# Narrower scores for the first query block of each sequence in a fused attention and MLP kernel

## The chip, the cores and the metric

The kernel runs on one core of one Trainium2 chip. The metric is the device time of one launch in microseconds. The engines are named as in the profile: PE is TensorE (matmuls), PEld its weight loads, DVE is VectorE, ACT is ScalarE, POOL is GpSimd, SP is the queue that issues most of the DMAs. Everything is computed in fp32 accuracy.

## The reference

Four sequences of 768 positions, eight heads of 64, attend to a window of the last 128 positions and to the first four positions ("sinks"). The result goes through an MLP with a softplus.

```python
scores = scale * np.matmul(q, k.transpose(0, 1, 3, 2))
is_sink = pos[None, :] < int(n_sink)
rel = pos[:, None] - pos[None, :]
keep = is_sink | ((rel >= 0) & (rel < int(window)))
scores = np.where(keep, scores, -1000000000.0)
a = np.exp(scores - np.max(scores, axis=-1, keepdims=True))
a = a / (np.sum(a, axis=-1, keepdims=True) + 1e-09)
attn = np.matmul(a, v)
# then, per position, with x of 512 numbers:
h = x @ w_in
g = np.maximum(h, 0.0) + np.log1p(np.exp(-np.abs(h)))
out = g @ w_out
```

Queries come in blocks of 128. A block needs the keys of its own block (up to the diagonal), of the block before it (beyond the diagonal), and the sinks. The first block of a sequence has no block before it.

## The kernel before

Work is cut into 12 chunks of 256 queries, three to a sequence: chunk 0, 3, 6 and 9 begin a sequence (`self.first`). A chunk has eight heads, counted on through the chunks, so that head 24 is the first of chunk 3. Each head has two query blocks, j = 0 and j = 1, and passes through these steps: `load` (DMA), `split` (rounded part and rest of q and k), `scores`, `softmax`, `normalise`, `weights_t` (transposes of the weights and their masking on GpSimd into `pt`), `values` (product with v and with the sinks' values `vs`), `out`. Every four heads, `sink_weights` and `sink` transpose the weights on the sinks (tile `ts`, line 281). The MLP's `up`, `softplus`, `gate`, `residue` and `down` of a chunk run eight heads later, between the attention steps of the next one.

The keys of a chunk lie in SBUF as key block, 8 sink keys, key block, 8 sink keys, key block. For query block j the scores are one stretch of 264 columns: the block before, the sinks, the own block. The softmax then copies the own block's scores over those of the block before wherever key position is not beyond the query's (`c.diag`), and goes on with 136 columns, 128 keys and 8 sinks. For the first block of a sequence, the layout holds block 0 twice, in the place of the block before too.

The chunks 0 and 1 are "exact": q and k are plain fp32, and a product is one matmul in the program, two records in the profile (line 227). From chunk 2 on q and k are split into parts rounded to fp32r, and a block's scores are two matmuls that add up in PSUM (lines 230 and 231). The rest of the kernel's large matmuls (lines 327, 333, 459, 496 to 498) are of the rounded kind as well; those of the MLP are the bulk of the work.

```python
mv = slice(j * KW, j * KW + 2 * P + NS)      # KW = 136, P = 128, NS = 8
nc.tensor.matmul(s[:], hi[:, st], hi[:, mv], start=True, stop=False)
nc.tensor.matmul(s[:], hi[:, st], kl[:, mv], start=False, stop=True)
...
nc.vector.copy_predicated(self.s[h, j][:, :P], c.diag[:], self.s[h, j][:, KW:])
```

The order on TensorE and on the SP queue is the order in which the program is written: a list by hand (`START`) for the first two chunks, and then one round per head with fixed strings of steps (`STEADY`). The rounds of a sequence's first heads also build the sinks' values on GpSimd (`sinks`). In the first 100 us or so the MLP's weights arrive, issued from ScalarE's queue, and are unpacked from 64-bit words and split by ScalarE, VectorE and GpSimd (lines 403, 48, 50, 52, 56), in the same queues as the attention's steps.

A score tile is a PSUM tile of 264 columns; two pools hold two buffers each, so scores of a later head wait until the softmax has read those of an earlier one.

Of the kernel before, what the change touches and what calls it, by code (L numbers as in the profile page):

```python
# [22 lines left out]
P = 128  # L23
NB = S // P
NS = 8
KW = P + NS
CH = 2
# [95 lines left out]
class _Attention:  # L123
# [93 lines left out]
    def scores(self, h):  # L217
        c, nc = self.c, self.c.nc
        ops = self.heads.pop(h)
        for j in range(CH):  # L220
            pool, tag = (c.ps_h, "h") if self.chunk == 0 and h % 2 else (c.ps_s, "s")
            s = pool.tile([P, 2 * P + NS], F32, tag=tag, name=f"s{self.chunk}_{h}_{j}")
            mv = slice(j * KW, j * KW + 2 * P + NS)
            st = slice(KC + j * P, KC + j * P + P)
            if self.exact:
                q, k = ops
                nc.tensor.matmul(s[:], q[:, j * P : j * P + P], k[:, mv], start=True, stop=True)  # L227
            else:
                hi, kl = ops
                nc.tensor.matmul(s[:], hi[:, st], hi[:, mv], start=True, stop=False)  # L230
                nc.tensor.matmul(s[:], hi[:, st], kl[:, mv], start=False, stop=True)  # L231
            self.s[h, j] = s

    def softmax(self, h):
        c, nc, chunk = self.c, self.c.nc, self.chunk
        g, hh = h // G, h % G
        if hh == 0:
            self.a[g] = c.ap.tile([P, G, CH, KW], F32, tag="a", name=f"a{chunk}_{g}")
            self.rc[g] = c.sp.tile([P, CH, G], F32, tag="rc", name=f"rc{chunk}_{g}")
        sm = c.sp.tile([P, CH], F32, tag="sm", name=f"sm{chunk}_{h}")  # L240
        self.sm[h] = sm
        for j in range(CH):
            nc.vector.copy_predicated(self.s[h, j][:, :P], c.diag[:], self.s[h, j][:, KW:])  # L243
        for j in range(CH):
            a = self.a[g][:, hh, j]
            k = (chunk * H + h) * CH + j
            nm = c.stats[:, k : k + 1]
            m = c.masks[min(self.i0 + j, 2)]
            nc.vector.tensor_tensor_reduce(a, self.s.pop((h, j))[:, :KW], m[:], -SCALE, BIG, ALU.add, ALU.min, nm)  # L249
            nc.scalar.activation(a, a, AF.Exp, bias=nm, scale=-1.0, accum_out=sm[:, j : j + 1])  # L250
# [653 lines left out]
```

## Time and profile before

| | |
|---|---|
| device time, median of 3 runs | 740.09 us (737.24 to 740.62) |
| span of the profiled execution | 735.7 us, 13883 instructions |
| TensorE busy | 699.7 us, 95% |
| VectorE busy | 552.6 us, 75% |
| ScalarE busy | 446.1 us, 61% |
| GpSimd busy | 400.7 us, 54% |
| score matmuls, lines 227, 230, 231 | 64, 160 and 160 records |
| copies, line 243 | 192, 49.1 us busy |

The profiled execution's own time is its span from the first to the last instruction, 735.7 us; no time around it is given with the profile. A row of a group view has the line, the engine, the operation, the tiles, the shapes and the count, then busy time and mean time of one record, then the idle time of the engine before these records and what ended it. Busy times on TensorE count overlapping records once and a record's length includes its way through the array, so the distance between two starts, from the view in order of time, says what a matmul costs. A piece of the chain of waits has its start, its length, the engine, tile and line.

### The profile page before, as it was taken

To read this page: it belongs to the slowest core of one execution; us is meant where nothing else is said; L and a number is where in the kernel's file an instruction comes from. 1 tells how busy PE (TensorE), PEld (TensorE's weight loads), DVE (VectorE), ACT (ScalarE), POOL (GpSimd) and SP (SyncE) were. 2 spreads that over 40 slices of the span, in tenths; PEclk is the share of its full clock that TensorE was granted. 3 is DMA by queue.
4 is the path that set the end of the run, shared out by engine and by line. 5 is a ranking of instruction groups with operands and counts; after the bars stand their busy time and mean duration, and the time that the engine had idled before them with its cause. 6 is when DMAs were issued, how large, how long until landed. Compare 5 with 4: busy or idle time off the path is not lost.

```text
span 735.7 us, 13883 instructions
## 1 busy us (share of the span) xinstructions
PE 699.7 (95%) x4489; PEld 624.8 (85%) x4489; DVE 552.6 (75%) x1608; ACT 446.1 (61%) x1098; POOL 400.7 (54%) x773
## 2 busy tenths in 40 slices
PE   4788899989999999998999999998999999999996
PEld 3567688979899999997899999997999999999995
DVE  5899997867877877876977887886887877754331
ACT  3577865655666666665666666665766756644331
POOL 4866476565555665665655655556655565553110
PEclk9899999999999999999999999999999999999999
DMA  8877611411321321321321322322222222100001
GB/s 291 310 255 235 187 40 48 126 46 44 98 67 49 105 61 54 93 63 42 92 74 49 95 69 57 95 60 61 62 74 77 83 61 76 58 13 0 30 1 35
DMA packets 40876, 63.22 MB, mean 86 GB/s; under 512 B 4634, under 2 KB 22362, under 8 KB 40794
## 3 DMA queue, kind: packets, MB, share of 16 engines
q1 hardware_dynamic: 36042, 45.47, 21.2%
q10 hardware_dynamic: 4752, 16.77, 6.5%
q8 instruction: 38, 0.62, 0.4%
q14 instruction: 44, 0.36, 0.2%
HBM read 55.93 MB, written 6.29 MB: 85 GB/s over the span
## 4 chain that ended last, share of the span: by engine, by line
PE 83%; DVE 6%; POOL 4%; ACT 3%; DMA 1%; issue 1%; ACTq 0%; SPq 0%; POOLq 0%; DVEq 0%
PE h L459 34%; PE acc L496 11%; PE acc L498 11%; PE acc L497 11%; PE x L333 6%; PE t L297 2%; PE s L230 2%; PE s L231 2%; PE x L327 2%; PE s L227 1%; ACT a L250 1%; POOL a L264 1%; DMA wo71r<-w 1%; POOL pt L308 1%; PE ts L281 1%
## 5 line engine op out<-in xcount | busy, mean ns | idle before, releaser
L459 PE MATMUL h<-xh,wi 128*128 128x256 f32 x1536 | 254.6, 289 | 0.0
L459 PEld LDWEIGHTS h<-xh,wi 128*128 128x128 f32 x1536 | 212.3, 192 | 1.2 <-issue 0.3
L459 PE MATMUL h<-xl,wi 128*128 128x256 f32 x768 | 154.9, 284 | 0.0
L496 PE MATMUL acc<-wo,gh 128*128 128x512 f32 x384 | 153.7, 400 | 0.0
L498 PE MATMUL acc<-wo,gl 128*128 128x512 f32 x384 | 151.7, 395 | 0.7 <-DVE gl L56 0.7
L497 PE MATMUL acc<-wo,gh 128*128 128x512 f32 x384 | 151.5, 395 | 0.0
L52 POOL TENSOR_SCALAR gh<-mt 128x512 fp32r<-128x512 f32 x91 | 56.5, 621 | 166.7 <-DVE mt L474 165.4
L466 ACT ACTIVATE mt<-h 128x512 f32<-128x512 f32 x96 | 57.2, 596 | 114.2 <-PE h L459 114.2
L459 PEld LDWEIGHTS h<-xl,wi 128*128 128x128 f32 x768 | 120.0, 192 | 0.0
L264 POOL TENSOR_SCALAR a<-a,rc 128x128 f32<-128x128 f32 x180 | 71.9, 411 | 87.1 <-DVE rc L257 78.8
L250 ACT ACTIVATE a<-a,stats 128x136 f32<-128x136 f32 x192 | 75.9, 396 | 39.1 <-DVE stats L249 39.0
L474 DVE SCALAR_TENSOR_TENSOR mt<-h,mt 128x512 f32<-128x512 f32 x96 | 65.9, 687 | 42.4 <-ACT mt L468 28.2
L498 PEld LDWEIGHTS acc<-wo,gl 128*128 128x128 f32 x384 | 72.8, 189 | 17.8 <-DVE gl L56 1.2
L496 PEld LDWEIGHTS acc<-wo,gh 128*128 128x128 f32 x384 | 72.8, 190 | 12.9 <-issue 0.4
L497 PEld LDWEIGHTS acc<-wo,gh 128*128 128x128 f32 x384 | 72.9, 190 | 9.3
L56 DVE TENSOR_TENSOR gl<-mt,gh 128x512 fp32r<-128x512 f32 x96 | 70.5, 734 | 4.4 <-POOL gh L52 4.0
L467 ACT ACTIVATE mt<-mt 128x512 f32<-128x512 f32 x96 | 60.8, 633 | 3.1
L468 ACT ACTIVATE mt<-mt 128x512 f32<-128x512 f32 x96 | 60.7, 633 | 3.0
L351 DVE TENSOR_TENSOR xt<-x,xt 64x256 f32<-64x256 f32 x80 | 33.2, 415 | 38.9 <-ACT xt L48 38.9
L243 DVE COPY_PREDICATED s<-diag,s 128x128 f32<-128x128 int32 x192 | 49.1, 289 | 15.4 <-PE s L231 11.9
L48 ACT CAST qkh<-qk 128x656 fp32r<-128x656 f32 x80 | 59.3, 741 | 0.4 <-DMA qk<-qk 0.4
L333 PE MATMUL x<-pt,vv 128*128 128x256 f32 (+1 forms) x216 | 48.7, 328 | 7.9 <-POOL pt L311 7.9
(183 smaller groups left out, 1234.9 us busy)
## 6 DMA issues: line engine op xcount, KB each, us to landing
qk<-qk SPq DMA_DIRECT2D x160, 164.0 KB, 3.0
vr<-v SPq DMA_DIRECT2D x32, 192.0 KB, 2.8
out<-o SPq DMA_DIRECT2D x24, 256.0 KB, 2.3
q<-q SPq DMA_DIRECT2D x8, 256.0 KB, 4.7
vr<-v SPq DMA_DIRECT2D x16, 128.0 KB, 2.1
k<-k SPq DMA_DIRECT2D x8, 200.0 KB, 4.9
wi00r<-w ACTq DMA_DIRECT2D x1, 511.8 KB
wi01r<-w ACTq DMA_DIRECT2D x1, 511.8 KB
```

What stands on the lines that cost most here:

```text
L48: nc.scalar.copy(out, in_)
L56: (nc.vector if eng == "V" else nc.gpsimd).tensor_tensor(out, a, b, ALU.subtract)
L250: nc.scalar.activation(a, a, AF.Exp, bias=nm, scale=-1.0, accum_out=sm[:, j : j + 1])
L264: (nc.vector if eng == "V" else nc.gpsimd).tensor_scalar(a, a, rc[:, j : j + 1], 0.0, ALU.mult, ALU.add)
L333: nc.tensor.matmul(x[:, :, o], w, pt[:, :, m], start=False, stop=n == 2, skip_group_check=True)
L459: nc.tensor.matmul(h[:, j], wt, x, start=k == 0, stop=k >= len(prods) - 2, skip_group_check=True)
L467: nc.scalar.activation(t[:], t[:], AF.Exp, scale=-1.0)
L468: nc.scalar.activation(t[:], t[:], AF.Ln, bias=1.0)
L474: nc.vector.scalar_tensor_tensor(t[:], h[:], 0.0, t[:], ALU.max, ALU.add)
L496: nc.tensor.matmul(acc[:], gh[:, j, q], wh, start=f == 0, stop=False, skip_group_check=True)
L497: nc.tensor.matmul(acc[:], gh[:, j, q], wl, start=False, stop=False, skip_group_check=True)
L498: nc.tensor.matmul(acc[:], gl[:, j, q], wh, start=False, stop=f == 2 * FP - 1, skip_group_check=True)
```

## The change

For the first query block of a chunk that begins a sequence, the matmuls compute 136 columns, the first copy of block 0 and the sinks, and the copy of the second over the first is left out. The PSUM tile keeps its size; loads, layout, masks and the softmax's remaining steps are as they were.

```diff
             s = pool.tile([P, 2 * P + NS], F32, tag=tag, name=f"s{self.chunk}_{h}_{j}")
-            mv = slice(j * KW, j * KW + 2 * P + NS)
+            w = KW if self.first and j == 0 else 2 * P + NS
+            mv = slice(j * KW, j * KW + w)
             st = slice(KC + j * P, KC + j * P + P)
+            o = s[:, :w]
             if self.exact:
                 q, k = ops
-                nc.tensor.matmul(s[:], q[:, j * P : j * P + P], k[:, mv], start=True, stop=True)
+                nc.tensor.matmul(o, q[:, j * P : j * P + P], k[:, mv], start=True, stop=True)
             else:
                 hi, kl = ops
-                nc.tensor.matmul(s[:], hi[:, st], hi[:, mv], start=True, stop=False)
-                nc.tensor.matmul(s[:], hi[:, st], kl[:, mv], start=False, stop=True)
+                nc.tensor.matmul(o, hi[:, st], hi[:, mv], start=True, stop=False)
+                nc.tensor.matmul(o, hi[:, st], kl[:, mv], start=False, stop=True)
             self.s[h, j] = s
...
-        for j in range(CH):
+        for j in range(1 if self.first else 0, CH):
             nc.vector.copy_predicated(self.s[h, j][:, :P], c.diag[:], self.s[h, j][:, KW:])
```

On TensorE, at the first head of chunk 3 (tile names are `s` with head, block and a number; `hi` and `kl` are the tiles `qkh` and `kl`), the order before was:

```order
L230 MATMUL s_0_0_1884<-qkh_0_1776 128x264
L231 MATMUL s_0_0_1884<-kl_0_1779,qkh_0_1776 128x264
L230 MATMUL s_0_1_1887<-qkh_0_1776 128x264
L231 MATMUL s_0_1_1887<-kl_0_1779,qkh_0_1776 128x264
L496 MATMUL acc_0_1700<-wo_691,gh_2_1714 128x512
```

and with the change it is:

```order
L232 MATMUL s_0_0_1876<-qkh_0_1768 128x136
L233 MATMUL s_0_0_1876<-kl_0_1771,qkh_0_1768 128x136
L232 MATMUL s_0_1_1879<-qkh_0_1768 128x264
L233 MATMUL s_0_1_1879<-kl_0_1771,qkh_0_1768 128x264
L498 MATMUL acc_0_1692<-wo_683,gh_2_1706 128x512
```

The places are the same; two of four score matmuls are narrower. Every later line number of the program moves by two, so that line 243 becomes 245. On VectorE, at the first head of the program, before (L249 is the masked reduction of a block's scores):

```order
L243 COPY_PREDICATED s_0_0_172<-diag,s_0_0_172 128x128
L243 COPY_PREDICATED s_0_1_174<-diag,s_0_1_174 128x128
L249 ISA a_0_178,stats<-s_0_0_172,mask_141 128x136
L249 ISA stats 128x1
L249 ISA a_0_178,stats<-s_0_1_174,mask_142 128x136
```

and with the change:

```order
L245 COPY_PREDICATED s_0_1_174<-diag,s_0_1_174 128x128
L251 ISA a_0_178,stats<-s_0_0_172,mask_141 128x136
L251 ISA stats 128x1
L251 ISA a_0_178,stats<-s_0_1_174,mask_142 128x136
L251 ISA stats 128x1
```

One copy of two is gone, and the remaining one still stands ahead of the reduction of block j = 0. On the other engines and on the DMA queues nothing moves.

## The prediction

> **What bounds the kernel now.** I read four views: the page's busy times and chain of waits, then stretches of time, then single TensorE records, then the start of the chain. The page first:
>
> ```profile
> PE 699.7 (95%) x4489; PEld 624.8 (85%) x4489; DVE 552.6 (75%) x1608; ACT 446.1 (61%) x1098; POOL 400.7 (54%) x773
> PE 83%; DVE 6%; POOL 4%; ACT 3%; DMA 1%; issue 1%; ACTq 0%; SPq 0%; POOLq 0%; DVEq 0%
> ```
>
> TensorE carries the end. But the average hides two regimes, which the view by stretches shows (columns: start and end, length, then PE, PEld, DVE, ACT, POOL busy with counts, granted clock, DMA share, GB/s):
>
> ```profile
> 10.00:20.00 10.00, 5.85 (x23) 4.28 (x24) 5.80 (x29) 6.24 (x23) 3.76 (x10) 0.78 1.01 377
> 17.00:20.00 3.00, 2.62 (x9) 2.05 (x10) 1.53 (x5) 2.89 (x9) 0.00 (x0) 0.50 1.03 413
> 20.00:30.00 10.00, 9.09 (x43) 5.87 (x42) 9.23 (x38) 5.26 (x20) 8.74 (x12) 0.88 0.84 310
> 30.00:40.00 10.00, 7.02 (x34) 4.47 (x32) 9.19 (x31) 5.49 (x19) 8.32 (x15) 1.00 0.78 276
> 90.00:100.00 10.00, 10.00 (x73) 8.81 (x72) 9.80 (x26) 6.77 (x15) 4.18 (x8) 1.00 0.19 52
> ```
>
> From 10 to 20 us no engine is full: the engines wait for each other in turn, partly at half clock (0.50). From 20 us VectorE is full (9.23, 9.19) and GpSimd nearly. From about 90 us TensorE never stops. So a shorter matmul pays in the first 20 us and after 90 us, a dropped VectorE copy pays before 90 us and almost nowhere after.
>
> **The change part by part.** It shortens the scores of query half j=0 in chunks 0, 3, 6 and 9 from 264 to 136 columns and drops their copies; no instruction changes place. The rows concerned, by shape:
>
> ```profile
> L230 PE MATMUL s<-qkh 128*128 128x264 f32 x160 | 43.7, 292 | 0.0
> L231 PE MATMUL s<-kl,qkh 128*128 128x264 f32 x160 | 42.6, 286 | 0.0
> L227 PE MATMUL s<-k,q 128*128 128x264 f32 x64 | 20.5, 457 | 9.2 <-DMA q<-q 5.6 <-DVE stats L249 2.5 <-PE s L227 0.6
> L459 PE MATMUL h<-xh,wi 128*128 128x256 f32 x1536 | 254.6, 289 | 0.0
> L243 DVE COPY_PREDICATED s<-diag,s 128x128 f32<-128x128 int32 x192 | 49.1, 289 | 15.4 <-PE s L231 11.9
> ```
>
> *Rounded scores (chunks 3, 6, 9): 3 chunks x 8 heads x 2 products = 48 matmuls.* A record's mean (292 ns) includes its latency; what it costs is the distance to the next start:
>
> ```profile
> 183.12 0.29 PE L230 MATMUL s<-qkh 128*128 128x264 f32 x1
> 183.24 0.29 PE L231 MATMUL s<-kl,qkh 128*128 128x264 f32 x1
> 183.37 0.29 PE L230 MATMUL s<-qkh 128*128 128x264 f32 x1
> 183.49 0.28 PE L231 MATMUL s<-kl,qkh 128*128 128x264 f32 x1
> 183.62 0.40 PE L496 MATMUL acc<-wo,gh 128*128 128x512 f32 x1
> 183.85 0.40 PE L497 MATMUL acc<-wo,gh 128*128 128x512 f32 x1
> 184.08 0.39 PE L498 MATMUL acc<-wo,gl 128*128 128x512 f32 x1
> ```
>
> Four of 264 columns take 0.50 us, 0.125 each (0.12 to 0.13), and one of 512 takes 0.23. That is (0.23 - 0.125) / 248 = 0.42 ns a column, so 128 columns fewer would give 0.054 back, if streaming were all. It isn't: each matmul has a weight load of its own, and the loads have a width and a pace too:
>
> ```profile
> L230 PEld LDWEIGHTS s<-qkh 128*128 128x128 f32 x160 | 30.5, 190 | 0.9 <-issue 0.3
> L327 PEld LDWEIGHTS x<-sk,vsf 128*64 128x64 f32 x32 | 3.2, 139 | 7.7 <-ACT sk L48 3.3 <-issue 2.6 <-DVE xl L56 1.3
> 144.15 0.19 PEld L230 LDWEIGHTS s<-qkh 128*128 128x128 f32 x1
> 144.25 0.19 PEld L231 LDWEIGHTS s<-kl,qkh 128*128 128x128 f32 x1
> 144.38 0.19 PEld L230 LDWEIGHTS s<-qkh 128*128 128x128 f32 x1
> ```
>
> 64 columns of weights fewer make a load 190 - 139 = 51 ns shorter, 0.8 ns a column; 128 columns then hold the loader some 0.10 us, and the closest pair here, behind a short matmul, is 0.10 to 0.11 apart. The next load starts with the matmul before it, so a matmul of 136 columns still lasts until the next weights are in. I expect a spacing of 0.117, 0.008 less than now: 48 x 0.008 = 0.4 us. The bounds: streaming alone, 48 x 0.054 = 2.6 us; nothing, if 0.125 is already the load's pace. I take the value next to the load rows, since the 0.10 to 0.11 is a measured distance of these same loads. The Trainium skill, page "TensorE: Matmul & The Clock Gate", section "LDWEIGHTS (loading the stationary operand)", says a load costs its columns divided by 1.2 GHz, which is an estimate of 107 ns here; by that rule the gain would be 48 x (125 - 107) = 0.9 us at most. The trace agrees with the pace (0.10 to 0.11).
>
> *Exact scores (chunk 0, 8 heads).* A plain fp32 product is two records (64 for 32 products). Warm, four records fit between these two starts, 0.89 / 4 = 0.22 each:
>
> ```profile
> 24.12 1.06 PE L227 MATMUL s<-k,q 128*128 128x264 f32 x4
> 25.01 0.38 PE L297 MATMUL t<-ident,a 128*128 128x128 f32 x2
> ```
>
> and these are the places where they, and the copies of chunk 0, stand on the chain of waits:
>
> ```profile
> 5.62 3.61 PE s L227 x8
> 9.86 2.04 PE s L227 x8
> 13.82 0.39 DVE s L243 x2
> 16.28 0.39 DVE s L243 x2
> 17.38 0.58 PE ts L281 x2
> 17.96 1.76 PE s L227 x4
> 20.15 1.76 PE s L227 x4
> 27.64 0.38 DVE s L243 x2
> ```
>
> At half clock a record is 1.76 / 4 = 0.44. Scaled by 136/264 it becomes 0.227, saving 0.213; warm 0.22 becomes 0.12 (the load's pace again), saving 0.10. On the chain: heads 0 and 1, four cold records, 0.85; heads 2 and 3, four warm, 0.40; a copy of head 3 and one of head 4, half of 0.39 each, 0.39. That is 1.64 us by 17 us, where the first stretches show no other engine full, so I count all of it. Behind it stand heads 5 and 6 (four cold records, 0.85) and one copy (0.19), but there VectorE and GpSimd are full and have work of their own; I count 0.2 of this 1.04. Term: 1.8 us. Upper bound 2.7 (all); lower bound 0, if a weight transfer or GpSimd holds the next step anyway. In the new VectorE order the copy of j=1 still stands ahead of the j=0 reduction, so j=0 is not released earlier by itself.
>
> *Dropped copies of chunks 3, 6, 9: 24.* Records overlap, so each frees 0.39 / 2 = 0.195 us, 4.7 us together. I cost them at nothing: TensorE's 10.00 of 10 covers them. If that cover were gone they would give up to those 4.7. One kind of place has none, where TensorE waits for a chain with VectorE in it:
>
> ```profile
> 185.86 0.40 DVE s L243 x2
> 192.48 0.62 PE L333 MATMUL x<-pt,vv 128*128 128x512 f32 x2 [0.39 <-POOL pt L311]
> 162.68 1.01 PE L333 MATMUL x<-pt,vv 128*128 128x256 f32 x2 [2.38 <-POOL pt L311]
> ```
>
> The wait of 0.39 at 192.48 hangs on a chain that passes head 29's copies; it and its twin a batch later shrink by 0.2 each: 0.4 us. The 2.38 at 162.68 ends with GpSimd, behind ScalarE and the sink tiles; no copy is on it, and it stays.
>
> **The sum**: 1.8 + 0.4 + 0.4 = 2.6 us off the profiled execution's span of 735.7, giving 733.1. The median of the runs shown, 740.09, is 4.4 above that span (what lies around it, and the spread of executions, 737.24 to 740.62); I leave that as it is: 740.1 - 2.6 = **737.5 us**.
>
> **The rivals.** *Streaming sets the pace.* If a second weight load can hide further ahead, 48 x 0.054 = 2.6 replaces 0.4: 4.8 us in all, 735.3. For it: in every row here but a few the load is hidden, so its own pace is seldom seen. Against it: the 0.10 to 0.11 between loads. The skill's same page, section "Back-to-back issue gap", gives columns / 2.4 GHz + 2.5 ns for a matmul by itself, an estimate of 59 ns at 136 columns, and warns that it under-counts where loads are paired; no run here shows 136 columns.
>
> *Narrow rounded matmuls fall back to the slow form (slower than before).* All rounded matmuls of the trace have 256 columns or more (L230, L231, L459 above; the narrower ones are plain or transposes). If under 256 they ran like plain fp32, two records of twice the columns, each would cost 2 x (0.22 x 136/264 + 0.01) = 0.25, 0.125 more than now: 48 x 0.125 = 6.0 us lost against 2.2 gained, 743.9. From 2.2 / 48 = 0.046 us extra a matmul on, this decides the sign. For it: nothing narrower was ever run here. Against: the type, not the width, tells the two forms apart in the trace (L227 has 264 columns and is slow).
>
> *The start swallows its gain.* TensorE already runs at 0.50 between 17 and 20 us after an idle stretch; with shorter matmuls it idles more and may be slow once more. In ten such microseconds some 3 us of chain records would double, +3 against -2.6: 740.5. Likewise, if GpSimd (8.74 of 10) is the true pace from 20 us, the 1.8 falls to nothing: 739.3.
>
> **How the numbers follow.** Forecast 0.60, streaming 0.13, slow form 0.13, swallowed start 0.14. Half a percent, 3.7 us, is about what a measurement of this kernel can tell from no change. Under 736.4: a quarter of the forecast (the start's upper bound, 2.7, with the load rule's 0.9) and most of streaming, with the scatter of executions: 0.30. Over 743.8: half of the slow form and little else: 0.10. Within: 0.60. The range takes in streaming's 735.3 with some scatter below, and the swallowed start's 740.5 with some above, and leaves most of the slow form out: 734.0 to 742.0.
>
> **What would show it.** Right: the j=0 rounded rows of 136 columns start 0.11 to 0.12 apart, 0.12 to 0.125 for j=1; the first weight load of chunk 0's sink transposes comes 1.6 us earlier than 17.4; steady rounds of eight heads take as long as before. Wrong: spacings of 0.07 (streaming) or 0.25 in two records (slow form); a further half-clock stretch before 40 us; or a shift at 17 us that is gone by 90 us.

## The result and the profile after

| | before | changed |
|---|---|---|
| device time, median of 16 runs each, same chip | 740.17 us (737.24 to 742.22) | 735.9 us (733.78 to 737.71) |
| ratio, 95% interval | | 0.9946 (0.9935 to 0.9958) |
| profiled execution: span, and its own time | 735.7 us, none on record | 735.4, 737.14 us |

The change makes the kernel 0.54% faster by the ratio, 4.0 us (3.1 to 4.8); the medians lie 4.3 us apart. The forecast was 737.5 us: the direction is right, the time lies in the range, and the gain is 1.4 to 1.7 us larger than the 2.6 that were summed. Ratios, here and below, are taken over all executions but three that lay far off (776, 1758 and 1769 us), so a gain worked out from a ratio can differ by about 1 us from the distance of two medians.

The two spans differ by 0.3 us only. That of the changed kernel is the 14th of its 16, while that of the kernel before was a fast one: all executions with both numbers on record lie 1.66 to 1.85 us above their span, which puts it near 737.5 us (an estimate), and only two of its 16 are under that. So the two traces may not be subtracted. They are read below place by place, with further profiles of the same code beside them.

The page of the changed kernel (engine busy times, shares of the chain of waits, the costliest group of copies):

```profile
PE 702.0 (95%) x4489; PEld 626.3 (85%) x4489; DVE 545.9 (74%) x1576; ACT 446.2 (61%) x1098; POOL 402.0 (55%) x773
PE 85%; DVE 4%; ACT 3%; POOL 3%; DMA 2%; issue 1%; ACTq 0%; SPq 0%; POOLq 0%
L245 DVE COPY_PREDICATED s<-diag,s 128x128 f32<-128x128 int32 x160 | 41.8, 288 | 18.0 <-PE s L233 13.5
```

32 copies are gone (192 to 160) and VectorE works 6.7 us less. Its share of the chain fell from 6% to 4%, and that of the DMAs rose from 1% to 2%, which comes up again below. TensorE keeps all 4489 matmuls and carries the chain as before (85%). (In the changed kernel the score lines are 229, 232 and 233, the masks 310 and 313, the products with v and with the sinks' values 335 and 329, `up` 461, `down` 498 to 500: two more than before each.)

The groups by shape show the narrowed matmuls:

```profile
L233 PE MATMUL s<-kl,qkh 128*128 128x136 f32 x24 | 6.6, 274 | 0.0
L232 PE MATMUL s<-qkh 128*128 128x136 f32 x24 | 5.7, 238 | 0.0
L229 PE MATMUL s<-k,q 128*128 128x136 f32 x16 | 5.5, 442 | 6.4 <-DMA q<-q 5.6 <-DVE stats L251 0.8
```

A rounded matmul of half the columns still has a record of 238 and 274 ns (292 and 286 before). What counts is the distance between starts. The same place as in the prediction, head 29 of chunk 3, single TensorE records (start, duration) and below them the weight loads:

```profile
182.31 0.23 PE L232 MATMUL s<-qkh 128*128 128x136 f32 x1
182.37 0.27 PE L233 MATMUL s<-kl,qkh 128*128 128x136 f32 x1
182.48 0.34 PE L232 MATMUL s<-qkh 128*128 128x264 f32 x1
182.65 0.29 PE L233 MATMUL s<-kl,qkh 128*128 128x264 f32 x1
182.78 0.40 PE L498 MATMUL acc<-wo,gh 128*128 128x512 f32 x1
```

```profile
182.19 0.19 PEld L232 LDWEIGHTS s<-qkh 128*128 128x128 f32 x1
182.31 0.19 PEld L233 LDWEIGHTS s<-kl,qkh 128*128 128x128 f32 x1
182.42 0.19 PEld L232 LDWEIGHTS s<-qkh 128*128 128x128 f32 x1
182.53 0.19 PEld L233 LDWEIGHTS s<-kl,qkh 128*128 128x128 f32 x1
```

The four matmuls take 0.47 us from the first start to the step behind them, 0.50 before. The loads come every 0.11 us. The first narrow matmul starts the second after 0.06, but the third then has to wait for its weights: the distances are 0.06, 0.11, 0.17 and 0.13. With the step before them included, 18 of the 24 heads take 0.586 to 0.592 instead of 0.612; the other six, beside transposes, save 0.01 to 0.02. So 24 heads give at most 24 x 0.025 = 0.6 us.

The start, by stretches (start, end, length, then PE, PEld, DVE, ACT and POOL busy, granted clock, DMA share, GB/s) and by TensorE records (the bracket names the idle time before and its end):

```profile
10.00:20.00 10.00, 6.82 (x23) 4.69 (x22) 5.11 (x25) 5.37 (x21) 3.73 (x10) 1.00 0.97 366
20.00:30.00 10.00, 8.51 (x42) 5.23 (x41) 9.83 (x36) 5.48 (x21) 9.36 (x13) 1.00 0.91 335
```

```profile
5.64 3.00 PE L229 MATMUL s<-k,q 128*128 128x136 f32 x8 [5.64 <-DMA q<-q]
9.24 3.03 PE L229 MATMUL s<-k,q 128*128 128x136 f32 x8 [0.60 <-DVE stats L251]
12.87 1.70 PE L229 MATMUL s<-k,q 128*128 128x136 f32 x4 [0.17 <-DVE stats L251]
17.59 0.59 PE L283 MATMUL ts<-ident,sa 128*32 128x128 f32 x2 [3.01 <-ACT a L264]
```

In these rows each group mixes narrow and wide scores. Heads 0 and 1 (5.64) take 3.00 us where they took 3.61. But heads 2 and 3 (9.24) take 3.03 where they took 2.04 with all their columns: they ran at half clock here, and at full clock in the trace of before. The clock column says 1.00 for 10 to 20 us all the same, so the clock is read here from the length of the records: the same eight take 1.67 us in the 200-column kernel of part 2 below. So the sink transposes, forecast 1.6 us earlier than 17.38, come at 17.59.

### The profile page after: what moved, and what is told of

It is laid out like the page before. It is cut to its first block, busy times and chain, and to the rows that moved or that the text cites. A ratio compares the mean times of both kernels' runs of the same rounds, so it can differ in the third digit from the quotient of the medians.

```text
span 735.4 us, 13844 instructions
## 1 busy us (share of the span) xinstructions
PE 702.0 (95%) x4489; PEld 626.3 (85%) x4489; DVE 545.9 (74%) x1576; ACT 446.2 (61%) x1098; POOL 402.0 (55%) x773
## 4 chain that ended last, share of the span: by engine, by line
PE 85%; DVE 4%; ACT 3%; POOL 3%; DMA 2%; issue 1%; ACTq 0%; SPq 0%; POOLq 0%
PE h L461 35%; PE acc L498 11%; PE acc L500 11%; PE acc L499 11%; PE x L335 6%; PE t L299 3%; PE s L232 2%; PE s L233 2%; PE x L329 2%; ACT a L252 1%; DMA wi00r<-w 1%; DMA wo71r<-w 1%; PE ts L283 1%; POOL vs L159 1%; POOL a L266 1%
## 5 line engine op out<-in xcount | busy, mean ns | idle before, releaser
L245 DVE COPY_PREDICATED s<-diag,s 128x128 f32<-128x128 int32 x160 | 41.8, 288 | 18.0 <-PE s L233 13.5
```

## The experiments

All ratios are against the kernel before on the same chip, with 95% intervals. No kernel leaves out work of the reference; where one adds columns or matmuls that nobody reads, it is said.

**1. The change in four parts.** Chunk 0 alone, both edits:

```diff
-            w = KW if self.first and j == 0 else 2 * P + NS
+            w = KW if self.chunk == 0 and j == 0 else 2 * P + NS
...
-        for j in range(1 if self.first else 0, CH):
+        for j in range(1 if self.chunk == 0 else 0, CH):
```

> Only chunk 0 has the narrower scores and the dropped copies; chunks 3, 6 and 9 are as before. Theory A (the parts add up: an earlier start, two waits behind VectorE gone, matmuls paced by their weight loads): 0.9 to 1.8 us less than the kernel before, and TensorE's full stretch begins 0.8 us earlier in the profile. Rival B (most of the 4.3 us is the clock: each wait for the sinks' values near 160, 330 and 500 us can be followed by 1.4 us lost at half clock, and the earlier start moves these waits against the gate's beat): 3 us or more from this part alone, or nothing, in steps of 1.4. Rival C (VectorE is the limit throughout): 1 us at most.

Chunks 3, 6 and 9 alone, both edits:

```diff
-            w = KW if self.first and j == 0 else 2 * P + NS
+            w = KW if self.first and self.chunk and j == 0 else 2 * P + NS
...
-        for j in range(1 if self.first else 0, CH):
+        for j in range(1 if self.first and self.chunk else 0, CH):
```

> Only chunks 3, 6 and 9 have the narrower scores and the dropped copies; chunk 0 is as before. Theory A: 24 heads x 0.025 us of matmuls (0.6) and two waits of 0.55 us near 192 and 362 us gone (1.1): 1.0 to 1.7 us less. Rival B: under 0.7 us, or a step of 1.4 more or less. Rival C: 3 us.

All four chunks, the copies dropped, the scores wide as before:

```diff
-            w = KW if self.first and j == 0 else 2 * P + NS
+            w = 2 * P + NS
```

> Only the copies are dropped, in all four chunks; the scores stay 264 columns wide. Theory A: the two waits of 0.55 us go, and the start gains 0.2 to 0.6: 1.1 to 1.7 us less; four score matmuls of a head take 0.61 us from the start of the one before to the one after, as before. Rival B: no sum of parts, steps of 1.4. Rival C: 3.5 us or more, nearly the whole gain.

All four chunks, the scores narrow, the copies kept (the block is copied onto itself, which changes nothing in it):

```diff
-        for j in range(1 if self.first else 0, CH):
-            nc.vector.copy_predicated(self.s[h, j][:, :P], c.diag[:], self.s[h, j][:, KW:])
+        for j in range(CH):
+            e = 0 if self.first and j == 0 else KW
+            nc.vector.copy_predicated(self.s[h, j][:, :P], c.diag[:], self.s[h, j][:, e : e + P])
```

> Only the scores are narrower, in all four chunks; for j=0 of a first block VectorE still does a copy of the same size, of the block onto itself. Theory A: 24 x 0.025 = 0.6 us in the matmuls and 0.4 to 0.9 at the start: 1.0 to 1.5 us less; the waits of 0.55 us near 192 and 362 us stay. Rival B: no sum of parts, steps of 1.4. Rival C: under 0.7 us.

| kernel | median, us | ratio | gain by the ratio, us |
|---|---|---|---|
| before, same chip | 740.35 | | |
| chunk 0 alone | 736.68 | 0.9945 (0.9927 to 0.9963) | 4.1 (2.7 to 5.4) |
| chunks 3, 6, 9 alone | 738.67 | 0.9988 (0.9968 to 1.0008) | 0.9 (-0.6 to 2.4) |
| copies dropped alone | 739.4 | 0.9986 (0.9965 to 1.0007) | 1.0 (-0.5 to 2.6) |
| narrow scores alone | 737.31 | 0.9961 (0.9945 to 0.9977) | 2.9 (1.7 to 4.1) |

Most of the gain sits in chunk 0 and in its narrower matmuls. Theory A, the sum of parts with 0.9 to 1.8 us for chunk 0, is out, and what rival B gave for this part, 3 us or more, is what came. The dropped copies by themselves can't be told from no change, though up to 2.6 us isn't excluded; VectorE is not the main thing that the change relieves. The later chunks by themselves can't be told from no change either, which agrees with the 0.6 us of the records.

**2. 200 columns.** In chunks 3, 6 and 9, 200 columns instead of 136, the last 64 unused; chunk 0 as in the change:

```diff
-            w = KW if self.first and j == 0 else 2 * P + NS
+            w = KW if self.chunk == 0 and j == 0 else 200 if self.first and j == 0 else 2 * P + NS
```

> The changed kernel, but with 200 columns instead of 136 for the first blocks of chunks 3, 6 and 9 (64 of them unused). If the weight loads set the pace below some 250 columns, four score matmuls of a head and the step before them take as long as with 136, 0.586 us from the start of the one before to the start of the one after. If streaming sets it, half of the 0.027 us gained is lost again and more: 0.60 or above, with 0.08 to 0.09 between the first two starts in either case. The time stays within 0.5 us of the changed kernel's either way.

The time is 734.69 us, ratio 0.9936 (0.9913 to 0.9958), some 0.9 us under the changed kernel where 0.5 was expected; five executions (733.29 to 735.8) can't make more of that. Head 29 again, TensorE records:

```profile
178.83 0.26 PE L232 MATMUL s<-qkh 128*128 128x200 f32 x1
178.93 0.27 PE L233 MATMUL s<-kl,qkh 128*128 128x200 f32 x1
179.04 0.30 PE L232 MATMUL s<-qkh 128*128 128x264 f32 x1
179.18 0.28 PE L233 MATMUL s<-kl,qkh 128*128 128x264 f32 x1
179.29 0.39 PE L498 MATMUL acc<-wo,gh 128*128 128x512 f32 x1
```

0.46 us from the first start to the step behind, and 0.58 with the step before: no longer than with 136 columns (0.47 and 0.59). So in these heads 64 columns more cost nothing, and streaming doesn't set the pace up to 200 columns; the weight loads, 0.10 to 0.13 us apart here, do. That is the row that separates the two readings; the total time alone couldn't. The Trainium skill, page "TensorE: Matmul & The Clock Gate", section "LDWEIGHTS (loading the stationary operand)", gives a load its columns divided by 1.2 GHz, an estimate of 107 ns here, and the loads of this trace lie around it.

**3. The clock at the start.** The kernel before, with extra matmuls on the identity that nobody reads, 8 ahead of the first scores and 10 ahead of the first sink transposes, so that TensorE idles less there:

```diff
+def _warm(c, n):
+    t = c.ps_t.tile([P, CT], F32, tag="t", name="warm%d" % n)
+    for _ in range(n):
+        c.nc.tensor.matmul(t[:, :P], c.ident[:], c.ident[:], start=True, stop=True)
...
+        _warm(c, 8)
         for part in c.START.split():
+            if part == "K0":
+                _warm(c, 10)
```

> The kernel before, with 8 extra matmuls of the identity on itself ahead of the first scores (TensorE is idle there until 5.6 us) and 10 more in the idle stretch ahead of the first sink transposes (13.4 to 17.4 us); their output is read by nobody. Theory D (the changed kernel gains mostly because chunk 0's plain fp32 records run at half clock in most executions, 0.44 instead of 0.22 us, so that each narrowed one saves 0.21): the first records now run at full clock, and the kernel before loses 2 to 3 us of its 740.3 by this alone. Theory E (the start gains by the narrower records whatever the clock): under 1 us, or slower by the extra matmuls.

and the changed kernel with the same lines:

> The changed kernel with the same extra matmuls. Theory D: against the kernel before with them it gains only what is left at full clock, some 0.8 us of the start and 1 us later: 1.5 to 2.5 us, where the change alone gained 4.3. Theory E: the gap between the two stays at 3.5 us or more.

The kernel before falls from 739.67 to 736.77 us, ratio 0.9954 (0.9937 to 0.997): 2.9 us by the medians and 3.4 by the ratio, for 18 matmuls whose output nobody reads. The changed kernel with them takes 735.38 us, 0.9948 (0.9929 to 0.9967), no better than without. So the gap between the two is 0.4 us by the ratios and 1.4 by the medians: theory E's 3.5 is out, and the gap is, if anything, smaller than the 1.5 to 2.5 of theory D. The TensorE records of the kernel before with the extra matmuls:

```profile
5.87 2.49 PE L227 MATMUL s<-k,q 128*128 128x264 f32 x8
9.01 2.02 PE L227 MATMUL s<-k,q 128*128 128x264 f32 x8 [0.65 <-PE s L227]
16.55 0.38 PE L281 MATMUL ts<-ident,sa 128*32 128x128 f32 x2 [1.18 <-DVE sa L269]
```

Heads 0 and 1 take 2.49 us instead of 3.61, and the sink transposes come 0.8 earlier than 17.38. With the clock up, the narrow scores bring nothing more by the time of head 8: its scores start at 25.39 us here, and at 25.47 and 25.35 in the two narrow kernels with the same extra matmuls (the second is the last of part 5). So at the start the change buys back part of what half clock costs, and little else.

**4. Both kernels once more, unchanged,** since one profile of each had proved too few:

> The kernel before once more, for a second profile of it. Theory D: the first profile was of an execution at the fast end (735.7 of span, where the median execution is near 738.5), with chunk 0's records at full clock from 8.8 us; a usual execution keeps them at half clock to 12 us or later, and its head 8 starts its scores at 29 us or later instead of 27.5. Otherwise: full clock from 9 us again, and the span within 0.5 us of 738.5 all the same.

> The changed kernel once more, for a second profile and for its ratio beside the others: 0.9946 again, within 0.002. Theory D: the head 8 starts its scores by 27 us at whichever clock, since its narrow records cost 0.23 at half clock and 0.12 at full.

They take 739.47 us, 0.9994 (0.9974 to 1.0014), and 735.59 us, 0.9939 (0.9918 to 0.9959); spans 737.2 and 734.4. The expected late clock of the kernel before (half speed to 12 us or later) was not met: it rose at 10.2 us, and head 8's scores started at 28.21, not at 29 or later.

With these there are four profiles in which chunk 0 is wide (the two of before, chunks 3, 6, 9 alone, copies alone) and seven in which it is narrow and nothing else moves before 120 us (the two of the change, chunk 0 alone, narrow scores alone, 200 columns, and the two with moved sinks of part 5). Three marks in them, in us; the third is the same run of 24 `up` matmuls in the chain of waits, 120.51 in the first trace:

| mark | wide: each | narrow: each | means, and gain |
|---|---|---|---|
| first sink transposes | 17.4, 17.7, 17.7, 19.3 | 17.6, 17.5, 17.8, 17.7, 16.3, 17.6, 16.9 | 18.0 and 17.3: 0.7 |
| head 8's scores | 27.5, 28.2, 28.1, 29.6 | 27.0, 26.9, 27.7, 27.1, 25.7, 26.9, 26.9 | 28.4 and 26.9: 1.5 |
| `up` at 120 | 120.5, 120.9, 121.0, 122.8 | 119.7, 118.7, 118.7, 118.9, 117.8, 119.0, 118.1 | 121.3 and 118.7: 2.6 |

Profiles of one kind lie up to 2.3 us apart at a mark, so a gain is good to half a microsecond or so. About half of the first 1.5 us comes at and behind the sink transposes, where heads 5 and 6 run at half clock with fewer columns (1.76 us on the chain before, 1.33 in the changed kernel for one). The other 1.1 us come where no instruction was changed. At 49 us TensorE has waited some 2 us for ScalarE's copy of the sink weights. In the kernel before, and then in the second profile of the changed kernel:

```profile
49.08 0.65 PE L327 MATMUL x<-sk,vsf 128*64 128x256 f32 x2 [2.18 <-ACT sk L48]
51.53 1.20 PE L459 MATMUL h<-xh,wi 128*128 128x256 f32 x4
55.23 1.05 PE L227 MATMUL s<-k,q 128*128 128x264 f32 x4
```

```profile
48.16 0.65 PE L329 MATMUL x<-sk,vsf 128*64 128x256 f32 x2 [1.95 <-ACT sk L48]
49.80 0.72 PE L461 MATMUL h<-xh,wi 128*128 128x256 f32 x4
52.76 1.05 PE L229 MATMUL s<-k,q 128*128 128x264 f32 x4
```

The same 49 us of work: four `up` matmuls take 1.20 us after the wait in one and 0.72 in the other, and the next scores follow the wait by 6.15 and by 4.60. Behind the wait TensorE ran at half clock in all five profiles with a wide chunk 0 (6.1 us from wait to scores each, the one with extra matmuls among them), and in one of nine with a narrow one (the first profile of the changed kernel). Why an earlier arrival avoids it isn't shown: the waits are as long (1.9 to 2.2 us) with the fall as without.

**5. The wait for the sinks' values.** At 159 us, and again 170 and 340 us later, TensorE waits for GpSimd, which builds the sinks' values `vs` ahead of a head's masks. TensorE and GpSimd in the changed kernel:

```profile
159.09 0.28 PE L329 MATMUL x<-sk,vs 128*128 128x256 f32 x1
161.76 1.08 PE L335 MATMUL x<-pt,vv 128*128 128x256 f32 x3 [2.39 <-POOL pt L313]
162.64 0.63 PE L498 MATMUL acc<-wo,gh 128*128 128x512 f32 x1
163.06 0.63 PE L499 MATMUL acc<-wo,gh 128*128 128x512 f32 x1
```

```profile
156.68 0.60 POOL L151 TENSOR_SCALAR vsh<-vsr 64x128 fp32r<-64x128 f32 x1
158.61 1.09 POOL L159 TENSOR_TENSOR vs<-vsh,hmask 64x256 fp32r<-64x256 f32 x1
160.24 0.40 POOL L310 TENSOR_SCALAR_AFFINE_SELECT pt<-th 128x256 fp32r<-128x256 f32 x1
```

The masks on which the second product waits start at 160.24, behind the `vs` work. And the wait is followed by half clock again: matmuls of 512 columns start 0.42 us apart, not 0.23. First the sinks' values were only built two rounds earlier:

```diff
-        "J": (sinks(0), 2),
+        "J": (sinks(0), 4),
```

> The changed kernel with the sinks' values of a new sequence built two rounds earlier on GpSimd, so that the products of its first head do not wait 2.5 us for them (near 160, 330 and 500 us). If these waits, and the half clock that follows them (1.4 us each), are real losses: 3 x 2.5 = 7.5 us and up to 4.2 more, 724 to 729 us. If other work on GpSimd or ScalarE ends last there anyway, the waits shrink only to 1 or 2 us each: 2 to 4 us less.

734.86 us, 0.9949 (0.9929 to 0.9969), as good as the change alone: the wait moved a round ahead (behind the products at 144.6, 313.7 and 484.3 us) and was 2.15 there, where the 2 to 4 us expected did not come either. Then the values were loaded three rounds ahead and built behind the masks of the round instead of ahead of them:

```diff
-                if g == 0 and k:
+                if g == 0 and k == c.EXACT:
                     att[k].load_sinks()
...
+    def sink_load(i):
+        k = i // H
+        if i % H == 0 and k < n and att[k].first:
+            att[k].load_sinks()
...
-        "J": (sinks(0), 2),
-        "j": (sinks(1), G - 1),
+        "J": (sinks(0), 3),
+        "j": (sinks(1), G - 2),
+        "Z": (sink_load, 3),
...
-            for part in "JjGL" + c.STEADY[i % H == 0]:
+            for part in "ZGL" + c.STEADY[i % H == 0].replace("W", "WJj"):
```

> The changed kernel with the sinks' values of a new sequence loaded three rounds ahead and built on GpSimd behind a round's masking instead of ahead of it. If what TensorE waits for there is only the place of these five instructions in GpSimd's queue: the three waits of 2.5 us shrink below 0.5 us, and with them goes the half clock behind them: 6 to 11 us less than the changed kernel, 725 to 730 us. If GpSimd's other work that is now behind them ends last instead: waits of 1 to 2.5 us at another round, and less than 3 us gained.

725.74 us, 0.9813 (0.979 to 0.9835). The same place:

```profile
157.53 0.28 PE L329 MATMUL x<-sk,vs 128*128 128x256 f32 x1
158.09 0.73 PE L335 MATMUL x<-pt,vv 128*128 128x256 f32 x3 [0.28 <-POOL pt L313]
158.66 0.40 PE L498 MATMUL acc<-wo,gh 128*128 128x512 f32 x1
158.89 0.40 PE L499 MATMUL acc<-wo,gh 128*128 128x512 f32 x1
```

From `vs` product to mask product 0.56 us instead of 2.67, and no half clock behind (0.23 between starts). In all profiles but those with moved sinks' values, the 40 records behind this wait take either 5.7 to 5.8 us or 7.1 to 7.4, so half clock is easy to tell. Against the changed kernel on the same chip, 735.59, that is 9.9 us, as expected: 3 x 2.1 = 6.3 from the waits, and up to 3 x 1.4 = 4.2 from the slow stretches behind them, which are absent here at all three places. This kernel beats both. With the extra matmuls of part 3 on top:

> The same, with the extra matmuls of the identity ahead of the first scores and of the first sink transposes. Theory D: the narrow records at full clock save another 0.1 us each for some ten of them on the chain, 0 to 1.5 us less than without.

724.94 us, 0.98 (0.9777 to 0.9823): not to be told from the one without.

## Why the prediction was right or wrong

**The pace of the rounded matmuls: right, 0.4 forecast and 0.6 measured.** The mean distance of the four is 0.117, the value taken. The rows expected one by one (0.11 to 0.12 for j=0) are off: the short matmul hands its time to the next load, so it reads 0.06 and 0.11, and then 0.17. The rivals on this point fall: streaming alone would have given 64 columns a price, and they have none; no narrow matmul fell into two records of 0.25 us.

**The start: the step that failed, and luck in the total.** "On the chain: heads 0 and 1, four cold records, 0.85; heads 2 and 3, four warm, 0.40; a copy of head 3 and one of head 4 ... That is 1.64 us by 17 us." By 17 us the means differ by 0.7, and by 0.3 if the one late profile on the wide side (19.3) is left out. The sum took each record's speed from one execution and held it fixed. It isn't fixed: in five of the seven narrow profiles the clock rose later, and heads 2 and 3 lost there (3.03 for 2.04 us) what heads 0 and 1 gained. That part of the rival "the start swallows its gain" happened, and so did its sign, a further half-clock stretch before 40 us.

A second thing held the next step, one that the prediction's lower bound had named, "if a weight transfer or GpSimd holds the next step anyway". ScalarE issues the weight DMAs itself (line 370 in the changed kernel), in one order with its exponentials. In the second profile of the changed kernel, VectorE's statistics of head 3 and the chain of waits to the sink transposes:

```profile
14.44 0.08 DVE L251 DVE_READ_ACCUMULATOR2_ANT stats<- 128x1 f32 x1
```

```profile
8.03 6.63 DMA wi00r<-w
14.68 0.33 ACTq L370
15.11 0.90 ACT a L252 x4
```

The exponentials start 0.6 us after their statistics are there (0.1 elsewhere), behind a DMA issue that, by the chain, waited for an earlier weight transfer. In five of the seven narrow profiles the chain to the sink transposes passes such an issue. It costs 0.5 to 1.0 us in three of them and under 0.1 in the other two; in the four wide profiles it costs nothing. What each of the two things takes of the 1.64 in the mean isn't separated.

Behind 17 us the sum counted "0.2 of this 1.04"; the marks show 0.8 there (from 0.7 to 1.5). VectorE and GpSimd were full in that stretch, but the four cold records of heads 5 and 6 stood on the chain all the same. And 1.1 us came where the sum had no term, from a half-clock stretch at 51 us that mostly stays away. So 1.8 was forecast, with 2.7 as the upper bound, and 2.6 is what the marks give at 120 us, for other reasons than those of the sum. That the whole came out near the forecast is luck as far as this term goes.

**"The wait of 0.39 at 192.48 hangs on a chain that passes head 29's copies; it and its twin a batch later shrink by 0.2 each: 0.4 us": wrong as told.** The wait is gone altogether in the changed kernel, and also where the copies are kept or the later chunks are left as they were. It occurs exactly where one VectorE instruction ahead of the copies is long. VectorE and then GpSimd in the kernel before, when the wait occurs (two more masks, at 183.36 and 183.61, stand between the first and the second GpSimd row):

```profile
183.05 2.20 DVE L56 TENSOR_TENSOR qkh<-qk,qkh 64x256 fp32r<-64x256 f32 x1
```

```profile
183.00 0.40 POOL L308 TENSOR_SCALAR_AFFINE_SELECT pt<-th 128x256 fp32r<-128x256 f32 x1
183.97 0.29 POOL L311 TENSOR_SCALAR_AFFINE_SELECT pt<-tl 128x128 fp32r<-128x128 f32 x1
184.23 0.74 POOL L56 TENSOR_TENSOR vv<-vr,vv 128x256 fp32r<-128x256 f32 x1
```

and the same two places with chunk 0 alone changed, when it doesn't:

```profile
179.79 0.73 DVE L56 TENSOR_TENSOR qkh<-qk,qkh 64x256 fp32r<-64x256 f32 x1
```

```profile
179.75 0.40 POOL L310 TENSOR_SCALAR_AFFINE_SELECT pt<-th 128x256 fp32r<-128x256 f32 x1
180.12 0.55 POOL L313 TENSOR_SCALAR_AFFINE_SELECT pt<-th 128x128 fp32r<-128x128 f32 x1
```

In the first, VectorE's subtraction starts 0.05 us after GpSimd's first mask and ends at 185.25, when five GpSimd instructions are through (184.97). In the second it is done in 0.73, and the second mask takes 0.55 instead of 0.29. This fits the Trainium skill, page "SBUF — State Buffer", section "SBUF: two separate sides": VectorE with two inputs from SBUF and GpSimd share a pair of ports, and whoever has it keeps it for its whole instruction while the other stands still. The trace agrees that one of the two stands still; that the loser stood through five instructions and not one, the page doesn't say. The long ones, all six, start 0.04 to 0.07 us behind the mask; of the others at this place, those with the later chunks' copies in place start 0.01 to 0.04 behind it, and those without them 0.16 to 0.24. But the offset can't be the whole condition. A head later, in the kernel before, GpSimd's mask and VectorE's subtraction:

```profile
190.62 0.42 POOL L308 TENSOR_SCALAR_AFFINE_SELECT pt<-th 128x256 fp32r<-128x256 f32 x1
190.69 0.62 DVE L56 TENSOR_TENSOR qkh<-qk,qkh 64x256 fp32r<-64x256 f32 x1
```

Here the subtraction starts 0.07 behind the same kind of mask and takes 0.62, and it does so in every profile (0.06 to 0.08 behind, 0.61 to 0.62 long). GpSimd comes to this mask from scaling weights and not from the `vs` products. What decides isn't shown. What is shown is where it happens: at 6 of 15 such places in the five profiles that have VectorE's copies in the later chunks, and at none of 21 in the seven without them (the two profiles with the sinks' values built behind the masks left aside). So the dropped copies seem to matter here, by moving VectorE's start, and not by their own 0.2 us. The kernel before met the long instruction at 3 of 6 places in its two profiles, the changed kernel at 0 of 6. Each time costs 0.55 us (192.48 follows the product before it by 0.66, elsewhere by 0.12), so some 1.5 places x 0.55 = 0.8 us in the mean.

**The other dropped copies at nothing: right.** With the copies alone gone, 1.0 us (-0.5 to 2.6) is gained, 0.8 of which the held VectorE instruction would explain; the 4.7 that they would be worth uncovered is far off.

**"4.4 above that span ...; I leave that as it is."** An execution's own time lies 1.66 to 1.85 us above its span. The rest of the 4.4 is the distance of that execution, one of the fastest, from the median. The sum priced a typical execution with the records of a fast one, in which the clock rose earlier than in the other three wide profiles and two of the three half-clock stretches behind the sinks' values were absent.

**The account:** 2.6 (start) + 0.6 (matmuls) + 0.8 (VectorE's held instruction) = 4.0 us, against 4.0 to 4.3 measured. It isn't as closed as that looks: the first term is good to half a microsecond, and a further one is open. The half clock behind the sinks' values would go against the change by the profiles at hand: it occurs at 7 of 12 places where the later chunks are as before, and at 18 of 21 where they are changed and the wait stands where it stood. At 1.4 us each for three places this would take back some 1.2 us. Whether that is the change or chance, so few places can't tell.

## What to carry to other kernels

A matmul with 128 columns of weights gains little from fewer moving columns once the loads of the weights set the pace (0.6 us for 48 halved matmuls here): look at the distance between loads before pricing columns. Where TensorE idles for about 2 us, price the wait with the half clock behind it, and take durations from several profiled executions, since the one at hand may be among the fastest. A change of half a percent was worth less here than moving GpSimd's work behind the masks that TensorE waits for (9.9 us).

## What the runs showed of the hardware that was not expected

- Waits of 1.9 to 2.4 us of TensorE are often followed by some microseconds at half clock, which cost 1.4 to 1.5 us, in some executions and not in others with a wait of the same length. The Trainium skill, page "TensorE: Matmul & The Clock Gate", part "Part 1: The HAM clock gate", names an idle window of about 3.4 us for the fall; here half clock came after a wait of 1.92.
- The clock column can read 1.00 while the records run at half speed: 10 to 20 us of the changed kernel, where eight score records took 3.03 us that take 1.67 at full clock (200-column kernel, same place).
- One VectorE instruction that elsewhere takes 0.4 to 0.8 us took 2.20 us beside five GpSimd instructions in a row, and ended when they were through. A start 0.04 to 0.07 us behind the first of them went with it, but the same start a head later did not.
- Exponentials on ScalarE started 0.5 to 1.0 us late behind a DMA issue in ScalarE's own order that waited for an earlier transfer.
- 136 and 200 moving columns cost the same (0.59 and 0.58 us a head with the step before), in pairs of matmuls with 128 columns of weights each.
